# S5 state-space mix with a gated feed-forward: x's last 1024 tokens turned in 32 by 32 blocks on VectorE, parameters loaded on ScalarE's queue

## The chip, the cores and the metric

One core of one Trainium2 chip. The metric is the device time of one execution in microseconds (us), median of several runs. Engines are named TensorE (PE in the profile; PEld its weight loads), VectorE (DVE), ScalarE (ACT), GpSimd (POOL) and SyncE (SP); SP, ACT and POOL can issue DMA transfers.

## The reference: what is computed

x is one sequence of 2048 tokens with 448 features, all in bf16.

```python
g = sigmoid((x * gate_w).sum(-1, keepdims=True))
# a: a diagonal state-space layer, complex state of 448
Lam_bar = exp(exp(log_dt) * Lam)
Bu = einsum("bld,pd->blp", x, ((Lam_bar - 1) / Lam)[:, None] * Bmat)
h[t] = Lam_bar * h[t-1] + Bu[t]
a = 2 * einsum("blp,dp->bld", h, Cmat).real + x * Dskip
# b: a feed-forward, 448 -> 1792 -> 448
b = silu(x @ w1) @ w2
out = g * a + (1 - g) * b
```

## The kernel before

**Tiles.** The tokens go in four chunks of 512 (`tc`). For each chunk TensorE makes the "x products": 14 tiles F (x times w1, 128 of the 1792 columns each) and 7 tiles B (x times B, real and imaginary parts of the state in seven slots of 128 rows). Both need x turned, features on the partitions, in `xT`. The 448 features are held in four blocks of 128 rows that start at features 0, 128, 256 and 320, so the third and the fourth overlap by 64; the products take halves of 64 rows from them, two tiles at a time on the two halves of the array (`x_products`, L647; the matmul is L663).

**Turning x.** TensorE turns x by transposes against an identity into PSUM, and VectorE ("d") or ScalarE ("a") evicts it: chunk 0 in `x0_transposes` (L468), chunks 1 to 3 in `x_transposes` (L498): 32 transposes (L508) and two evictions of 128x1024 each. Chunk 1 is evicted "da", chunks 2 and 3 "aa" (L874, L879).

**The lanes.** The recurrence is made real by turning each state with its own angle (tables COS and SIN): `lanes(tc)` (L706) on VectorE multiplies the B products (U, in the tiles UG) by COS and SIN into H, runs seven scans along the 512 tokens (L736) into Gf, gets these as bf16 back into UG (by POOL's transfers, in the last chunk by ScalarE, L746), turns them back and leaves the result in H0 to H3 (L766, a subtraction). Each chunk starts from the last column of the one before. H3 is the last chunk's; before that its space holds B as loaded (`Bnat`), until `b_transposes` (L593) has turned it.

**Readouts.** `readout` (L786) multiplies H of 128 tokens by the weights CP (L795); VectorE adds the rest (L798) and SP stores it. `ffn2` (L768) makes the second feed-forward product (L774); ScalarE scales it (L780) and POOL adds it by a transfer.

**Parameters.** `parameters` (L529): three rows (log_dt, Lambda's parts) are loaded into `prm`, copied on VectorE (L538), turned by TensorE (L536), evicted (L540); POOL makes the exponential (L543), VectorE the angles from L544 on, and from these COS and SIN with ScalarE.

**What sets the order.** `Plan.order` (L104) schedules all operations by costs and priorities that the kernel gives them: TensorE keeps the written order, the other engines take whichever ready operation has the lowest priority number. `Waits` (L204) then makes one fixed list for each engine. Loads stand on SP's queue in the written order (xn0's first half, w1, the parameters, B, the last of w1, gate_w, Dskip, chunk 1 of x, w2, C, chunks 2 and 3 of x); ScalarE's queue has xn0's second half and two transfers of w1. w1's columns come in four cuts; of each cut, the feature blocks 0 to 2 and the overlapping block 3 are separate transfers (`load_w1`, L394). At the end the kernel's order is written out in L864 to L883: x products of all chunks, and between and behind them `ffn2` (G) and `readout` (C); the last are G(12..15), then C(12..15), which read H3.

Of the kernel before, what the change touches and what calls it, by code (L numbers as in the profile page):

```python
# [11 lines left out]
BF16 = DT.bfloat16  # L12
# [10 lines left out]
NOT = 5  # L23
NWARM = 6
NFILL = 2
XCOL = [0, 128, 256, 320]

TURN = 6.283184
# [248 lines left out]
def bass_gated_mix__ssm_conv_s5__dense_activation_silu__prompt_kernel(nc, A_x, A_Lambda_re, A_Lambda_im, A_B_re, A_B_im, A_C_re, A_C_im,  # L277
               A_log_dt, A_Dskip, B_x, B_w1, B_w2, gate_w, out):
    with ExitStack() as ctx:
# [3 lines left out]
        def sb(name, shape, dtype):  # L283
            return E(nc.sbuf_tensor(name, list(shape), dtype))
# [1 line left out]
        x2, out2 = A_x[0], out[0]  # L286

        xnat = sb("xnat", [128, NTB, D_MOD], BF16)
        xT = sb("xT", [128, 4, S_TOK], BF16)
        w1s = sb("w1s", [128, 4, F_FF], BF16)  # L290
        w2s = sb("w2s", [128, NFB, D_MOD], BF16)
        BT = sb("BT", [128, 4, 896], BF16)
# [94 lines left out]
        def load(q, dst, src, name, nbytes, prio=None, after=()):  # L387
            nl[0] += 1
            prio = nl[0] if prio is None else prio
            P.add(q, lambda e: e.dma_start(dst, src), list(after), name.split(), 0.6 if q == "pool" else 0.5, prio, sem(), nbytes, tag="ld " + name)  # L390
# [3 lines left out]
        def load_w1(q, k, a, b):  # L394

            cols = slice(w1cuts[k], w1cuts[k + 1])
            src = B_w1[320:448, cols] if a == 3 else B_w1[128 * a:128 * b, cols].rearrange("(b p) f -> p b f", p=128)
            load(q, w1s[:, 3, cols] if a == 3 else w1s[:, a:b, cols], src, " ".join(f"w1_{k}_{i}" for i in range(a, b)),
                 256 * (b - a) * (cols.stop - cols.start))

        for h, q in enumerate(("sp", "act")):
            load(q, xnat[:, 2 * h:2 * h + 2, :], x2[256 * h:256 * h + 256, :].rearrange("(b p) d -> p b d", p=128), f"xn0{h}", 256 * 896)
        load_w1("sp", 0, 0, 2)
        load_w1("act", 0, 2, 3)
        load_w1("act", 0, 3, 4)
        for k in range(1, len(w1cuts) - 2):
            load_w1("sp", k, 0, 3)
            load_w1("sp", k, 3, 4)
        for k, v in enumerate((A_log_dt, A_Lambda_re, A_Lambda_im)):
            load("sp", prm[k:k + 1, 0:448], v.rearrange("(o n) -> o n", o=1), f"prm{k}", 896)  # L410
        Bnat = H[3][:, :, 0:D_MOD]
        load("sp", Bnat[:, 0:3, :], A_B_re[0:384, :].rearrange("(b p) d -> p b d", p=128), "H3_0 H3_1 H3_2", 384 * 896)
        load("sp", Bnat[0:64, 3, :], A_B_re[384:448, :], "H3_3", 64 * 896)
        load("sp", Bnat[64:128, 3, :], A_B_im[384:448, :], "H3_3i", 64 * 896)
        load("sp", Bnat[:, 4:7, :], A_B_im[0:384, :].rearrange("(b p) d -> p b d", p=128), "H3_4 H3_5 H3_6", 384 * 896)
        btn = {s: [f"BT{s}_{h}" for h in range(2)] for s in range(7)}
        load_w1("sp", len(w1cuts) - 2, 0, 3)
        load_w1("sp", len(w1cuts) - 2, 3, 4)
        for dst, src, name in ((gwb, gate_w, "gwb"), (dkb, A_Dskip, "dkb")):
            load("sp", dst[:, :], src.rearrange("(o n) -> o n", o=1).partition_broadcast(128).rearrange("p o n -> p (o n)"),  # L420
                 name, 128 * 896)
# [46 lines left out]
        def x0_transposes(q0, part, who):  # L468

            tk = Ps(2)  # L470

            def mm(pe):
                for q in (q0, q0 + 1):
                    for k in range(2):
                        o = ((q - q0) * 2 + k) * 64
                        for h in range(2):
                            p = slice(64 * h, 64 * h + 64)
                            r = pe.transpose(bk(tk, h).bitcast(BF16)[:, o:o + 64], xnat[p, 2 * part + k, XCOL[q]:XCOL[q] + 128], ident[p, p])  # L478
                return r
            PE(mm, [f"xn0{part}", "ident"], [tk], 4 * 0.054, "xT0")  # L480
            for h in range(2):
                src = lambda h=h: bk(tk, h).bitcast(BF16)[:, 0:256].rearrange("p (q b n) -> p q b n", q=2, n=64)
                dst = xT[:, q0:q0 + 2, 256 * part:256 * part + 256].rearrange("p q (b h n) -> p q b h n", h=2, n=64)[:, :, :, h, :]
                names = [f"xT0_{q}{part}{h}" for q in (q0, q0 + 1)]
                if who[h] == "d":
                    DVE(lambda e, src=src, dst=dst: e.tensor_copy(dst, src()), [tk], names, 0.28, 0, "xTe")  # L486
                else:
                    ACT(lambda e, src=src, dst=dst: e.activation(dst, src(), AF.Copy), [tk], names, act_cost(256), 0, "xTe")
# [4 lines left out]
        x0_transposes(2, 1, "dd")  # L493

        xn_of = {tc: {q: [f"xT{tc}_{h}" for h in range(2)] for q in range(4)} for tc in range(1, NCH)}
        xn_of[0] = {q: [f"xT0_{q}{part}{h}" for part in range(2) for h in range(2)] for q in range(4)}

        def x_transposes(tc, who):  # L498

            tk = Ps(2)  # L500

            def mm(pe):
                for q in range(4):
                    for b in range(4):
                        o = (q * 4 + b) * 64
                        for h in range(2):
                            p = slice(64 * h, 64 * h + 64)
                            r = pe.transpose(bk(tk, h).bitcast(BF16)[:, o:o + 64],  # L508
                                             xnat[p, 4 * tc + b, XCOL[q]:XCOL[q] + 128], ident[p, p])
                return r  # L510
            PE(mm, [f"xn{tc}", "ident"], [tk], 16 * 0.035, f"xT{tc}")
            for h in range(2):
                src = lambda h=h: bk(tk, h).bitcast(BF16).rearrange("p (q b n) -> p q b n", q=4, b=4)
                dst = xT[:, :, tc * CH:(tc + 1) * CH].rearrange("p q (b h n) -> p q b h n", h=2, n=64)[:, :, :, h, :]
                if who[h] == "d":
                    DVE(lambda e, src=src, dst=dst: e.tensor_copy(dst, src()), [tk], [f"xT{tc}_{h}"], 0.69, 2.2, "xTe")
                else:
                    ACT(lambda e, src=src, dst=dst: e.activation(dst, src(), AF.Copy), [tk], [f"xT{tc}_{h}"], act_cost(1024), 2.2, "xTe")

        cosn = [f"COS{k}" for k in range(4)] + ["COSd"]  # L520
        sinn = [f"SIN{k}" for k in range(4)] + ["SINd"]
# [101 lines left out]
        def evict(pair, tk):  # L623

            kinds = [t[0] for t in pair]
            for k, n in ((0, 2),) if pair[0][:2] == pair[-1][:2] and len(pair) == 2 else ((0, 1), (1, 1))[:len(pair)]:
                kind, tc, a = pair[k]
                step = pair[k + 1][2] - a if n == 2 else 1
                sl = slice(a, a + step * (n - 1) + 1, step)
                names = [t[2] for t in pair[k:k + n]]  # L630
                src = (lambda: bk2(tk)) if n == 2 else (lambda k=k: bk(tk, k)[:, None, :])
                if kind == "F":
                    dst = aT[tc % 2][:, sl, :]
                    ACT(lambda e, src=src, dst=dst: e.activation(dst, src(), AF.Silu),  # L634
                        [tk, "tbl"], [f"aT{tc % 2}_{m}" for m in names], act_cost(512 * n), 2.5, "silu")
                    continue
                U, un = UG[tc % 2], f"U{tc % 2}_"
                dst = U[:, sl, :]
                if tc == 0:
                    DVE(lambda e, src=src, dst=dst: e.tensor_copy(dst, src()), [tk], [f"{un}{m}" for m in names], 0.15 + 0.53 * n, 2.6, "U")  # L640
                else:
                    ACT(lambda e, src=src, dst=dst: e.activation(dst, src(), AF.Copy), [tk], [f"{un}{m}" for m in names], act_cost(512 * n), 5, "U")  # L642
                if 3 in names:
                    load("pool", U[0:64, 7, :], U[64:128, 3, :], un + "7a", 65536, 9, [un + "3"])
                    load("pool", U[64:128, 7, :], U[0:64, 3, :], un + "7b", 65536, 9, [un + "3"])

        def x_products(tiles, fill={}, wait=()):  # L647
# [10 lines left out]
            def steps(k, h, a, z):  # L658
                def body(pe):
                    for n, cut in list(enumerate(part[h]))[a:z]:  # L660
                        for b, ((i, p0), tile) in enumerate(zip(cut, pairs[k])):
                            tc = tile[1]
                            r = pe.matmul(bk(toks[k], b), weights(tile, p0, p0 + 64, i), xT[p0:p0 + 64, i, tc * CH:(tc + 1) * CH],  # L663
                                          start=(h == 0 and n == 0), stop=(h == 1 and n == 2))
                    return r
                reads = [n for cut in part[h][a:z] for (i, _), tile in zip(cut, pairs[k])
                         for n in xn_of[tile[1]][i] + (w1n(tile[2], i) if tile[0] == "F" else btn[tile[2]])]
                return PE(body, list(dict.fromkeys(reads)), [toks[k]], (z - a) * PE_MM[512], f"{pairs[k][0][0]}{pairs[k][0][1]}")
# [192 lines left out]
        def C(*tbs):  # L861
# [3 lines left out]
        NH = 8  # L865
        K = NH // 2
        x_products(F(0, 0, NH) + B(0) + F(0, NH) + B(1),
                   {(1, 0): [parameters], (K - 2, 0): turn_b[:1], K - 2: turn_b[1:2], K - 1: turn_b[2:], 7: xt(1, "da") + [lambda: lanes(0)]}, [K - 2])
        gates(0)
        gates(1)  # L870
        lanes(1)
        for f in cp(0) + G(0, 1) + cp(1, 2) + G(2, 3) + cp(3):
            f()
        x_products(F(1) + F(2, 0, 1) + B(2), {2: xt(2, "aa")})  # L874
        gates(2)
        lanes(2)
        for f in G(4, 5, 6, 7) + C(0, 1, 2, 3):
            f()
        x_products(F(2, 1) + B(3) + F(3), {1: xt(3, "aa"), 9: [lambda: gates(3), lambda: lanes(3)]})  # L879
        for f in C(4, 5, 6, 7) + G(8, 9, 10, 11):  # L880
            f()
        for f in C(8, 9, 10, 11) + G(12, 13, 14, 15) + C(12, 13, 14, 15):
# [36 lines left out]
```

## Time and profile before

| | us |
|---|---|
| median of 3 runs | 141.97 (141.42, 141.97, 142.10) |
| the profiled execution | 141.25 |
| its span | 139.5 |
| TensorE busy in the span | 135.9 |
| VectorE busy | 122.0 |
| ScalarE busy | 90.3 |
| mean granted TensorE clock | 0.998 |

The span is the time from the first to the last instruction of the program; 1.75 us of the execution lie around it. The profile lists each engine's busy time, the chain of work that ended last (followed back from the last instruction to what released it), and groups of instructions by source line with what ended the idle time before them. The timeline lists instructions in order of time: start, duration, engine, line, what it writes and reads. Consecutive instructions on VectorE overlap slightly, so the distance between starts, not the duration, is what one costs its engine.

### The profile page before, as it was taken

The numbers are of one execution on the slowest core, as the hardware profiler recorded it, in microseconds if no ns is written. First come the engines' busy times: TensorE is split into PE (matmuls) and PEld (weight loads), VectorE is DVE, ScalarE is ACT, GpSimd is POOL, SyncE is SP. The second block draws the span as 40 slices with busy tenths as digits, with TensorE's granted clock in tenths as the row PEclk, the third lists the DMA queues.
The fourth block names the chain that finished last, engine by engine and source line by source line (L and its number), as shares of the span: only waits on it lengthen the run. The fifth ranks groups of instructions, "written<-read, shape, count | busy, mean of one in ns | idle before, by whom it ended". The sixth has DMA issues, their size and how long they took to land.

```text
span 139.5 us, 3000 instructions
## 1 busy us (share of the span) xinstructions
PE 135.9 (97%) x1201; PEld 67.0 (48%) x1201; DVE 122.0 (87%) x179; ACT 90.3 (65%) x157; POOL 39.2 (28%) x72
## 2 busy tenths in 40 slices
PE   7999999999999999999999999999999999999992
PEld 2445454455544544455544544444455555555561
DVE  0319999999999999999999999999999999997053
ACT  3349768999989999823694887799931268312300
POOL 7134040100248440227733001824000314022220
PEclk9999999999999999999999999999999999999999
DMA  4998999510156770104976200674202322323242
GB/s 136 337 294 243 363 320 238 177 42 0 31 79 94 129 110 1 38 15 73 157 131 155 38 5 0 95 133 79 38 4 97 66 33 36 83 83 61 40 94 71
DMA packets 17956, 14.71 MB, mean 105 GB/s; under 512 B 2835, under 2 KB 17814, under 8 KB 17942
## 3 DMA queue, kind: packets, MB, share of 16 engines
q0 software_dynamic: 6064, 5.51, 24.8%
q1 hardware_dynamic: 11318, 8.65, 20.7%
q10 hardware_dynamic: 560, 0.36, 0.8%
q8 instruction: 9, 0.15, 0.4%
q14 instruction: 5, 0.04, 0.1%
HBM read 7.17 MB, written 1.84 MB: 65 GB/s over the span
## 4 chain that ended last, share of the span: by engine, by line
PE 97%; DVE 0%; issue 0%
PE ps L663 46%; PE ps L774 31%; PE ps L795 15%; PE ps L463 2%; PE ps L508 1%; PE ps L478 1%; PE ps L814 1%; PE ps L604 1%; DVE ot L798 0%; PE ps L675 0%; PE ps L464 0%; PE ps L536 0%
## 5 line engine op out<-in xcount | busy, mean ns | idle before, releaser
L663 PE MATMUL ps<-xT,w1s 64*128 64x512 bf16 x392 | 48.5, 378 | 0.0
L774 PE MATMUL ps<-w2s,aT 128*128 128x448 bf16 x224 | 43.2, 353 | 0.0
L634 ACT ACTIVATE aT<-ps 128x1024 bf16<-128x1024 f32 (+1 forms) x30 | 28.7, 969 | 8.5 <-PE ps L663 8.4
L774 PEld LDWEIGHTS ps<-w2s,aT 128*128 128x128 bf16 x224 | 21.7, 98 | 20.4 <-ACT xnat L849 0.4
L663 PEld LDWEIGHTS ps<-xT,w1s 64*128 64x128 bf16 x392 | 19.7, 94 | 22.3 <-DVE xT L486 0.7
L663 PE MATMUL ps<-xT,BT 64*128 64x512 bf16 x196 | 25.8, 376 | 0.0
L782 POOL DMA_DIRECT2D xnat<-fe x16 | 14.1, 900 | 37.9 <-ACT fe L780 37.2
L780 ACT ACTIVATE fe<-ps,g 128x448 bf16<-128x448 f32 x16 | 10.1, 632 | 21.1 <-PE ps L774 21.0
L390 POOL DMA_DIRECT2D UG<-Gf x27 | 14.7, 549 | 20.9 <-DVE Gf L736 20.4
L736 DVE TENSOR_TENSOR_SCAN Gf<-rc,gin,H 128x512 f32<-128x512 f32 x14 | 17.2, 1268 | 0.0
L795 PE MATMUL ps<-CP,H 128*128 128x448 bf16 (+2 forms) x98 | 16.4, 326 | 0.0
L663 PEld LDWEIGHTS ps<-xT,BT 64*128 64x128 bf16 x196 | 10.8, 94 | 11.1 <-DVE Gf L562 0.2
L798 DVE SCALAR_TENSOR_TENSOR ot<-ps,g,xnat 128x448 bf16<-128x448 f32 (+2 forms) x18 | 10.8, 622 | 6.0 <-issue 4.6
L390 POOL DMA_DIRECT2D UG<-UG x8 | 4.8, 597 | 29.2 <-ACT UG L642 17.4
L704 DVE TENSOR_TENSOR H<-UG,COS 128x3584 bf16<-128x3584 bf16 (+4 forms) x10 | 12.6, 1266 | 0.0
L795 PEld LDWEIGHTS ps<-CP,H 128*128 128x128 bf16 x98 | 8.9, 98 | 7.5 <-DVE k L752 0.4
L642 ACT ACTIVATE UG<-ps 128x1024 bf16<-128x1024 f32 (+1 forms) x12 | 10.7, 923 | 1.4 <-PE ps L663 1.4
L842 ACT ACTIVATE junk<-xg 128x448 bf16<-128x448 bf16 x16 | 9.2, 574 | 2.1 <-DVE xg L704 2.0
L849 ACT ACTIVATE xnat<-xnat,g 128x448 bf16<-128x448 bf16 x16 | 9.8, 671 | 0.2
L704 DVE TENSOR_TENSOR PI<-UG,SIN 128x512 bf16<-128x512 bf16 (+2 forms) x13 | 9.1, 722 | 0.0
L704 DVE TENSOR_TENSOR PO<-UG,SIN 128x1536 bf16<-128x1536 bf16 (+1 forms) x8 | 8.7, 1087 | 0.1
L736 DVE TENSOR_TENSOR_SCAN Gf<-rc,gin,H2C 128x512 f32<-128x512 f32 x7 | 8.5, 1265 | 0.0
(102 smaller groups left out, 126.5 us busy)
## 6 DMA issues: line engine op xcount, KB each, us to landing
UG<-Gf POOLq DMA_DIRECT2D x21, 128.0 KB, 2.5
xnat<-fe POOLq DMA_DIRECT2D x16, 112.0 KB, 2.6
out_dram<-ot SPq DMA_DIRECT2D x15, 112.0 KB, 1.7
w2s<-in_B_w_dram SPq DMA_DIRECT2D x1, 1568.0 KB, 11.8
xnat<-in_A_x_dram SPq DMA_DIRECT2D x3, 448.0 KB, 6.1
w1s<-in_B_w_dram SPq DMA_DIRECT2D x1, 576.0 KB, 6.2
UG<-UG POOLq DMA_DIRECT2D x8, 64.0 KB, 2.2
H2C<-in_A_C_re_dram SPq DMA_DIRECT2D x2, 196.0 KB
```

Source lines behind the costliest of these rows:

```text
L390: P.add(q, lambda e: e.dma_start(dst, src), list(after), name.split(), 0.6 if q == "pool" else 0.5, prio, sem(), nbytes, tag="ld " + name)
L634: ACT(lambda e, src=src, dst=dst: e.activation(dst, src(), AF.Silu), [tk, "tbl"], [f"aT{tc % 2}_{m}" for m in names], act_cost(512 * n), 2 ...
L642: ACT(lambda e, src=src, dst=dst: e.activation(dst, src(), AF.Copy), [tk], [f"{un}{m}" for m in names], act_cost(512 * n), 5, "U")
L663: r = pe.matmul(bk(toks[k], b), weights(tile, p0, p0 + 64, i), xT[p0:p0 + 64, i, tc * CH:(tc + 1) * CH], start=(h == 0 and n == 0), stop=( ...
L704: DVE(lambda e: e.tensor_tensor(o, a, b, op), r, w, dve_cost(n, 2), prio, tag)
L736: DVE(lambda e, s=s, b=b, init=init: e.tensor_tensor_scan(Gf[:, s, :], rc[:, b:b + 1].to_broadcast([128, CH]), A[:, s, :], init, ALU.mult, ...
L774: r = pe.matmul(bk(tk)[:, 0:D_MOD], aT[tc % 2][:, fb, o:o + 128], w2s[:, fb, :], start=(fb == 0), stop=(fb == NFB - 1))
L780: ACT(lambda e: e.activation(f[:, :], bk(tk)[:, 0:D_MOD], AF.Copy, scale=g1[:, tb:tb + 1]), [tk, f"g1_{tc}"], [fn], act_cost(448, 1), 7, "fe")
L782: P.add("pool", lambda e: e.dma_start(Tb[:, tb, :], f[:, :], accum_op=ALU.add), [fn, f"Tb{tb}"], [f"Tb{tb}"], 0.94, 2, sem(), 115000, tag= ...
L795: r = pe.matmul(bk(tk)[:, 0:b - a], H[tc][:, s, o:o + 128], CP[:, s, a:b], start=(s == 0), stop=(s == NSLOT - 1))
L798: DVE(lambda e, tk=tk, a=a, b=b: e.scalar_tensor_tensor(ot[tb % NOT][:, a:b], bk(tk)[:, 0:b - a], g[:, tb:tb + 1], Tb[:, tb, a:b], ALU.mul ...
L849: ACT(lambda e, tb=tb: e.activation(Tb[:, tb, :], xnat[:, tb, :], AF.Copy, scale=g[:, tb:tb + 1]), [f"xd{tc}", f"g_{tc}"], [f"Tb{tb}"], ac ...
```

## The change

The parameter rows go on ScalarE's queue, and `parameters` is placed after the first two half tiles of x products (`(0, 0)`) instead of the next two (`(1, 0)`). Each cut of w1 is loaded as blocks 0 and 1, and blocks 2 and 3 in one transfer, whose second block starts 64 rows after the first. `xT` is laid out by chunk. Chunks 2 and 3 of x are no longer turned on TensorE: VectorE turns them in 32 by 32 blocks from `xnat` into the space of H3 (X32, four instructions a chunk), and SP carries the blocks to their rows of `xT` in 16 transfers of 32 partitions by 16 runs of 32 elements. On VectorE, chunk 2 has priority 15 after `PI_5` (of lanes 0), chunk 3 has 20.5 after `H0_0`. `UDVE` names all seven slots, so that line changes nothing.

```diff
+XT1 = "da"
+XPRIO = {2: 15, 3: 20.5}
+XBLK = (2, 3)
+XBEH = {2: "PI_5", 3: "H0_0"}
+UDVE = (0, 1, 2, 3, 4, 5, 6)
...
-        xT = sb("xT", [128, 4, S_TOK], BF16)
+        xT = sb("xT", [128, NCH, 4, CH], BF16)
...
+            n = cols.stop - cols.start
+            if b == 4:
+                src = bass.AP(B_w1.tensor, 128 * a * F_FF + cols.start, [[F_FF, 128], [(320 - 128 * a) * F_FF, 2], [1, n]])
...
-        load_w1("act", 0, 2, 3)
-        load_w1("act", 0, 3, 4)
+        load_w1("act", 0, 2, 4)
         for k in range(1, len(w1cuts) - 2):
-            load_w1("sp", k, 0, 3)
-            load_w1("sp", k, 3, 4)
+            load_w1("sp", k, 0, 2)
+            load_w1("sp", k, 2, 4)
         for k, v in enumerate((A_log_dt, A_Lambda_re, A_Lambda_im)):
-            load("sp", prm[k:k + 1, 0:448], v.rearrange("(o n) -> o n", o=1), f"prm{k}", 896)
+            load("act", prm[k:k + 1, 0:448], v.rearrange("(o n) -> o n", o=1), f"prm{k}", 896, 5)
...
+        def x_blocks(tc):
+            X32 = H[3][:, 0:4, :].rearrange("p m (q b i) -> p m q b i", q=4, i=32)
+            names = [f"X32_{k}" for k in range(4)]
+            held = [f"H3_{s}" for s in range(7)] + ["H3_3i"]
+            turned = [f"BT{s}_{h}" for s in range(7) for h in range(2)]
+            xs = xnat[:, 4 * tc:4 * tc + 4, :]
+            for k, (q0, q1, c, b0, b1) in enumerate(((0, 3, 0, 0, 2), (0, 3, 0, 2, 4), (3, 4, XCOL[3], 0, 2), (3, 4, XCOL[3], 2, 4))):
+                n = q1 - q0
+                src = xs[:, b0:b1, c:c + 128 * n].rearrange("p b (q m i) -> p b q m i", q=n, i=32)
+                dst = X32.rearrange("p m q b i -> p b q m i")[:, b0:b1, q0:q1, :, :]
+                DVE(lambda e, dst=dst, src=src: e.transpose(dst, src), [f"xn{tc}", XBEH[tc]] + turned, [names[k]], 0.15 + 256 * n / 960, XPRIO[tc], "xTd")
+            k = sem()
+            for g in range(4):
+                for m in range(4):
+                    to = xT[32 * m:32 * m + 32, tc, :, :].rearrange("p q (b g i) -> p (q b) g i", b=4, i=32)[:, :, g, :]
+                    P.add("sp", lambda e, to=to, g=g, m=m: e.dma_start(to, X32[32 * g:32 * g + 32, m, :, :, :].rearrange("p q b i -> p (q b) i")),
+                          names + held, [f"xT{tc}_{g}{m}"], 0.66, 400, k, 32768, tag="xTm")
...
-                   {(1, 0): [parameters], (K - 2, 0): turn_b[:1], K - 2: turn_b[1:2], K - 1: turn_b[2:], 7: xt(1, "da") + [lambda: lanes(0)]}, [K - 2])
+                   {(0, 0): [parameters], (K - 2, 0): turn_b[:1], K - 2: turn_b[1:2], K - 1: turn_b[2:], 7: xt(1, XT1) + [lambda: lanes(0)] + [lambda: x_blocks(2)] * (2 in XBLK)}, [K - 2])
...
+        if 3 in XBLK:
+            x_blocks(3)
-        x_products(F(1) + F(2, 0, 1) + B(2), {2: xt(2, "aa")})
+        x_products(F(1) + F(2, 0, 1) + B(2), {2: xt(2, "aa")} if 2 not in XBLK else {})
...
-        x_products(F(2, 1) + B(3) + F(3), {1: xt(3, "aa"), 9: [lambda: gates(3), lambda: lanes(3)]})
+        x_products(F(2, 1) + B(3) + F(3), {1: xt(3, "aa") if 3 not in XBLK else [], 9: [lambda: gates(3), lambda: lanes(3)]})
```

More of the change, by code (lines that the diff above doesn't have):

```diff
@@ L396, in load_w1 @@
             cols = slice(w1cuts[k], w1cuts[k + 1])
-            src = B_w1[320:448, cols] if a == 3 else B_w1[128 * a:128 * b, cols].rearrange("(b p) f -> p b f", p=128)
-            load(q, w1s[:, 3, cols] if a == 3 else w1s[:, a:b, cols], src, " ".join(f"w1_{k}_{i}" for i in range(a, b)),
-                 256 * (b - a) * (cols.stop - cols.start))
+            n = cols.stop - cols.start
+            if b == 4:
+                src = bass.AP(B_w1.tensor, 128 * a * F_FF + cols.start, [[F_FF, 128], [(320 - 128 * a) * F_FF, 2], [1, n]])
+            else:
+                src = B_w1[128 * a:128 * b, cols].rearrange("(b p) f -> p b f", p=128)
+            load(q, w1s[:, a:b, cols], src, " ".join(f"w1_{k}_{i}" for i in range(a, b)), 256 * (b - a) * n)
         for h, q in enumerate(("sp", "act")):
@@ L416, in bass_gated_mix__ssm_conv_s5__dense_activation_silu__prompt_kernel @@
         btn = {s: [f"BT{s}_{h}" for h in range(2)] for s in range(7)}
-        load_w1("sp", len(w1cuts) - 2, 0, 3)
-        load_w1("sp", len(w1cuts) - 2, 3, 4)
+        load_w1("sp", len(w1cuts) - 2, 0, 2)
+        load_w1("sp", len(w1cuts) - 2, 2, 4)
         for dst, src, name in ((gwb, gate_w, "gwb"), (dkb, A_Dskip, "dkb")):
@@ L482, in x0_transposes @@
                 src = lambda h=h: bk(tk, h).bitcast(BF16)[:, 0:256].rearrange("p (q b n) -> p q b n", q=2, n=64)
-                dst = xT[:, q0:q0 + 2, 256 * part:256 * part + 256].rearrange("p q (b h n) -> p q b h n", h=2, n=64)[:, :, :, h, :]
+                dst = xT[:, 0, q0:q0 + 2, 256 * part:256 * part + 256].rearrange("p q (b h n) -> p q b h n", h=2, n=64)[:, :, :, h, :]
                 names = [f"xT0_{q}{part}{h}" for q in (q0, q0 + 1)]
@@ L495, in bass_gated_mix__ssm_conv_s5__dense_activation_silu__prompt_kernel @@
         xn_of = {tc: {q: [f"xT{tc}_{h}" for h in range(2)] for q in range(4)} for tc in range(1, NCH)}
+        for tc in XBLK:
+            xn_of[tc] = {q: [f"xT{tc}_{g}{m}" for g in range(4) for m in range(4)] for q in range(4)}
         xn_of[0] = {q: [f"xT0_{q}{part}{h}" for part in range(2) for h in range(2)] for q in range(4)}
@@ L513, in x_transposes @@
                 src = lambda h=h: bk(tk, h).bitcast(BF16).rearrange("p (q b n) -> p q b n", q=4, b=4)
-                dst = xT[:, :, tc * CH:(tc + 1) * CH].rearrange("p q (b h n) -> p q b h n", h=2, n=64)[:, :, :, h, :]
+                dst = xT[:, tc, :, :].rearrange("p q (b h n) -> p q b h n", h=2, n=64)[:, :, :, h, :]
                 if who[h] == "d":
@@ L638, in evict @@
                 dst = U[:, sl, :]
-                if tc == 0:
+                if tc == 0 and a in UDVE:
                     DVE(lambda e, src=src, dst=dst: e.tensor_copy(dst, src()), [tk], [f"{un}{m}" for m in names], 0.15 + 0.53 * n, 2.6, "U")
@@ L662, in body @@
                             tc = tile[1]
-                            r = pe.matmul(bk(toks[k], b), weights(tile, p0, p0 + 64, i), xT[p0:p0 + 64, i, tc * CH:(tc + 1) * CH],
+                            r = pe.matmul(bk(toks[k], b), weights(tile, p0, p0 + 64, i), xT[p0:p0 + 64, tc, i, :],
                                           start=(h == 0 and n == 0), stop=(h == 1 and n == 2))
```

## The prediction

> **What bounds the kernel now.** I read the chain of waits first, to see whose work sets the end.
>
> ```profile
> PE 135.9 (97%) x1201; PEld 67.0 (48%) x1201; DVE 122.0 (87%) x179; ACT 90.3 (65%) x157; POOL 39.2 (28%) x72
> ...
> DVE  0319999999999999999999999999999999997053
> ...
> PE 97%; DVE 0%; issue 0%
> ```
>
> TensorE is the chain from 0.76 us to 136.73 us. VectorE, though off the chain, has "9" in every slice from the fourth to the 36th: a second engine with no spare time, until shortly before the end. So I looked next at where the two meet: in the chain's pieces in order of time, and in VectorE's timeline.
>
> ```profile
> 5.00 3.82 PE ps L663 x30
> 8.82 0.18 PE ps L536 x4
> ...
> 45.55 0.47 PE ps L508 x32
> ...
> 77.23 0.47 PE ps L508 x32
> ...
> 120.79 10.59 PE ps L774 x56
> 131.38 5.35 PE ps L795 x42
> ```
>
> ```profile
> 124.07 2.09 DVE L704 TENSOR_TENSOR H<-UG,COS 128x2048 bf16<-128x2048 bf16 x2
> 126.07 2.09 DVE L704 TENSOR_TENSOR H<-H,PO 128x2048 bf16<-128x2048 bf16 x2
> 132.80 0.69 DVE L798 SCALAR_TENSOR_TENSOR ot<-ps,g,xnat 128x448 bf16<-128x448 f32 x1 [4.64 <-issue]
> ```
>
> The last four readouts (L795, at 131.38) read what the last lane chunk leaves in H3. VectorE finishes that at 128.16, so it is **3.2 us ahead** of TensorE, and this is all the slack it has: from 10.38 to 128.16 its timeline shows no gap above 0.15 us. Any work added to VectorE eats this slack; any work taken from TensorE eats it too.
>
> **Taken from TensorE.** x's chunks 2 and 3 lose their 32 transposes each: 2 x 0.47 = 0.94 us of the chain. TensorE would reach the last readouts at 131.38 - 0.94 = **130.44**. ScalarE loses the four evictions that belong to them (1.95 and 1.93 us), worth nothing: TensorE never waits for ScalarE in the chain.
>
> **The parameters come earlier.** Of VectorE's and ScalarE's beginning:
>
> ```profile
> 8.16 0.17 DVE L538 COPY prm<-prm 3x64 bf16<-3x64 bf16 x1 [2.84 <-DMA prm<-in_A_Lambda_im_dram]
> 9.04 0.17 DVE L540 COPY pc<-ps 128x12 f32<-128x12 f32 x1 [0.71 <-PE ps L536]
> ...
> 10.38 0.16 DVE L544 SCALAR_TENSOR_TENSOR ph<-dtc,pc 128x4 f32<-128x4 f32 x1 [0.88 <-POOL dtc L543]
> ```
>
> ```profile
> 1.25 0.97 ACTq L390 DMA_DIRECT2D w1s<-in_B_w_dram  x2
> 2.25 1.28 ACT L457 ACT_TABLE_LOAD   x1 [2.25 <-issue]
> 4.06 1.00 ACT L488 ACTIVATE xT<-ps 128x256 bf16<-128x256 bf16 x3 [0.53 <-PE ps L478]
> ```
>
> ScalarE's queue now issues one w1 transfer instead of two (half of 0.97) and three parameter rows; SP took 0.93 us for these (3.75 to 4.68). That ends at 1.25 + 0.5 + 0.93 = 2.68, the table load at 3.99, and x's first eviction waits for TensorE until 4.06 in any case: no cost, with 0.07 us left; past that, TensorE's start would move one for one. The rows land about 6.2 (before: 8.16, 3.5 us after their last issue). TensorE turns them after 16 products instead of 30: 14 x 3.82/30 = 1.78 us earlier, at 7.04, after the rows and their copy. So L544 starts at 8.60, not 10.38. Part of this is lost: the first turned B block leaves TensorE at 10.85 as before, and with 1.78 us more in hand VectorE idles about 0.3 us for it; the third pair of B products (18.1, from the products counted back from 19.64) costs about 0.1. I take a **head start of 1.35 us** for the lanes (1.0 if more such waits come, 1.78 at most). SP issues everything behind the rows 0.93 us earlier, which nothing waits for. w1 moves the same bytes in as many transfers on SP: 0.
>
> **Added to VectorE: eight 32 by 32 transposes**, per chunk two of 768 and two of 256 elements in each partition. No row of before shows this operation. Rows at one element a cycle are nearest, since each element is read and written once without arithmetic in pairs: 128x512 f32 subtract (L527) goes 13.10 to 13.70, 0.60 us to the next start; the 1024 eviction from PSUM (L640) 15.24 to 16.37, 1.13. That is 0.07 + 1.04 ns an element: 0.87 and 0.34, so 2.42 us a chunk and **4.84** for both. Bounds: at the copy's pace (L565, 1536 in 0.45, 0.29 ns) 1.7; at the scan's (L736, 512 in 1.19, 2.3 ns) 9.6. Behind the first chunk's blocks on VectorE stand the rest of lanes 0 and CP's evictions: CP0 comes about 0.9 us later than now, while its bank is wanted at 34.4 (ready 32.5); CP3 is ready at 42.8, wanted about 44. Neither stops TensorE. Behind the second stand all of lanes 1 to 3.
>
> **Sum.** H3 is ready at 128.16 - 1.35 + 4.84 = 131.65, against TensorE's 130.44: the 0.94 us is turned into a wait in front of the last readouts. With 0.1 us from one engine to the next they start at 131.75 instead of 131.38, **0.37 us late**, and what follows (5.35 us of products, last store) is as before. 141.25 of the profiled execution becomes 141.62. That execution is 0.72 us under the median of the runs shown (141.97), so I forecast on the median: **142.3**.
>
> **The transfers.** Per chunk 16 transfers of 32 KB on SP, in 64-byte pieces: 8192. The first chunk's blocks follow PI_5: lanes start 26.0, blocks run 29.6 to 33.2 around CP0. TensorE wants chunk 2 at 50.1 (92 products after 40.15). So 16 issues and their pieces have 14.9 us, with 2 us for the last to land (stores take 1.7). SP's issues take 0.42 to 0.82 us (two 512-piece loads in 1.65): 6.7 to 13.1. For the pieces: the trace's packets of 128 B on SP's queue take 13 ns, 8192/16 x 13 = 6.7 us; all packets of the window 19 to 25:
>
> ```profile
> DMA packets 2515, 1.50 MB, mean 250 GB/s; under 512 B 1036, under 2 KB 2482, under 8 KB 2514
> ...
> q1 hardware_dynamic: 2450, 1.35, 95.1%
> ```
>
> 0.951 x 16 x 6 us / 2450 = 37 ns, so 19 us. I take the 128-byte row, nearest in size: landed about 43 to 48, hidden. Chunk 3 starts about 62.5 and is wanted at 81; its last four transfers stand on SP behind the first three stores (70 to 73): landed about 76, hidden. Stores wait behind the transfers meanwhile; five buffers cover that until about 102.
>
> **Rivals.**
> 1. *The transposes don't overlap with the next instruction* (slower). If each costs its full duration, by L527's 0.68 for 512 a fixed 0.15: 8 x 0.15 + 4.27 = 5.5 us. H3 at 132.3, 1.0 us late: 142.3 on the profiled execution, **143.0** on the median. It decides from 5.2 us for the eight on. [...] Against: every row shown overlaps by 0.07 to 0.08. [...]
> 2. *The transposes are cheap, or the head start is whole* (faster). Under 3.5 us for the eight (some 0.8 ns an element) H3 is no longer late: all of 0.94 is gained, **141.0** on the median. For: L565's copy moves 0.29 ns an element. Against: it is a copy of rows in order.
> 3. *Chunk 2 lands late* (slower). Over about 28 ns a piece, or 0.93 us an issue, TensorE stalls at 50.1. Up to 1.2 us of it vanishes in the wait for H3. At 37 ns: 54.1, a 4.0 us stall, last readouts at 134.4, 3.1 us late: **145** on the median. Against: those 37 ns belong to packets of 551 B on the mean.
>
> That the order is not as the diff says is excluded: VectorE's and TensorE's lists of after show it.
>
> **Chances.** Forecast 0.47, rival 1 0.25, rival 2 0.13, rival 3 0.12; 0.03 for a small stall unnamed. The range, 141.0 to 143.9, holds the first three and what lies between, and leaves out most of rival 3. About 0.5% (0.7 us) is what a measurement can tell from no change: faster 0.13, the same 0.46, slower 0.41.
>
> **What would show it.** In after, no transposes of chunks 2 and 3 on TensorE; L544's counterpart near 8.6; lanes 0 from about 26.0; transposes near 0.9 and 0.4 us; VectorE's last H3 subtraction ending near 131.7 without the gap in front of the last stores' evictions; and TensorE idle about 1.3 us before its last readouts, put down to VectorE, with no wait for a transfer at 50 or 81. Wrong it would be by a wait at 50 (rival 3), or by no wait before the last readouts (rival 2).

## The result, and the profile after

| | before | after |
|---|---|---|
| median, measured side by side | 141.71 (141.23 to 142.52, 10 runs) | 142.85 (142.23 to 143.93, 10 runs) |
| the profiled execution | 141.25 | 142.23 |
| its span | 139.46 | 140.43 |
| H3 ready (VectorE) | 128.16 | 131.34 |
| first of the last readouts (TensorE) | 131.22 | 131.40 |
| last eviction ends (VectorE) | 137.10 | 137.29 |
| from there to the end of the span | 2.36 | 3.14 |

After takes 1.0088 [1.0064, 1.0111] times as long as before: slower by 0.9%, where I had forecast 0.37 us (0.3%). The median lies in the forecast's range (141.0 to 143.9), but the loss of 1.14 us is three times the forecast one. In this table a stage's time is the start of its first instruction, which for the last readouts is 0.16 us ahead of the chain's 131.38, because the records of consecutive matmuls overlap. The two profiled executions differ by 0.98 us, as the medians do by 1.14, so the traces can be compared term by term.

The page of after, engines and chain:

```profile
PE 134.8 (96%) x1137; PEld 66.1 (47%) x1137; DVE 126.7 (90%) x187; ACT 86.9 (62%) x153; POOL 38.6 (27%) x72
...
DVE  0369999999999999999999999999999999999560
...
PE 4%; DVE 0%; issue 0%
```

TensorE lost 64 instructions and 1.1 us, VectorE gained eight instructions and 4.7 us. VectorE is busy earlier (its third slice is a 6 and not a 1), and its 9s end in the 37th slice, not the 36th. The chain of before was TensorE from 0.76 us on; now it breaks off after 4%. Its pieces in order of time (start, us, what):

```profile
131.35 0.05 issue
131.40 5.52 PE ps L824 x42
136.92 0.02 issue
136.94 0.35 DVE ot L827
```

The waits name what stands in front of 131.40, and a second stop of TensorE at 21.66 (engine, line, what it waited for: us in total, times, longest; a third, of 0.3 us at 4.79, belongs to the start):

```profile
PE ps L824 <- DVE H L733: 0.7, 1, 0.7
PE ps L692 <- ACT xT L527: 0.3, 1, 0.3
```

The first is the wait that the forecast saw coming: VectorE's last subtraction into H3. VectorE's timeline (start, duration), the start of the lanes in before and then after:

```profile
27.51 0.68 DVE L704 TENSOR_TENSOR H<-UG,COS 128x1024 bf16<-128x1024 bf16 x1
```

```profile
25.69 0.68 DVE L733 TENSOR_TENSOR H<-UG,COS 128x1024 bf16<-128x1024 bf16 x1
...
29.24 1.83 DVE L541 STREAM_TRANSPOSE H<-xnat 128x768 bf16<-128x768 bf16 x2
31.00 0.64 DVE L856 SCALAR_TENSOR_TENSOR CP<-ps,sc1s,ct 128x448 bf16<-128x448 bf16 x1
...
32.15 0.76 DVE L541 STREAM_TRANSPOSE H<-xnat 128x256 bf16<-128x256 bf16 x2
32.83 0.38 DVE L733 TENSOR_TENSOR H<-H,PI 128x512 bf16<-128x512 bf16 x1
...
129.25 2.09 DVE L733 TENSOR_TENSOR H<-H,PO 128x2048 bf16<-128x2048 bf16 x2
132.99 0.68 DVE L827 SCALAR_TENSOR_TENSOR ot<-ps,g,xnat 128x448 bf16<-128x448 f32 x1 [1.65 <-issue]
```

Two transposes of 768 elements run from 29.24 to the next start at 31.00, 0.88 us each; two of 256 from 32.15 to 32.83, 0.34 us each: 2.44 us for chunk 2. Chunk 3's four run from 59.45 to 61.86, 2.41 us: 4.85 for both. The lanes start at 25.69 (before: 27.51), and the idle time in front of the last readouts' first eviction fell from 4.64 to 1.65 us. The transposes are near the forecast; the lanes started earlier than it said.

The second stop was not forecast. ScalarE's timeline, its half of chunk 1's eviction in before, and then after, at the start and around chunk 1:

```profile
20.17 1.02 ACT L518 ACTIVATE xT<-ps 128x1024 bf16<-128x1024 bf16 x1
```

```profile
2.96 1.28 ACT L464 ACT_TABLE_LOAD   x1 [2.96 <-issue]
4.26 0.94 ACT L495 ACTIVATE xT<-ps 128x256 bf16<-128x256 bf16 x3
...
19.89 0.71 ACT L592 ACTIVATE COS<-Gf,hpi 128x512 bf16<-128x512 f32 x1
20.50 1.01 ACT L527 ACTIVATE xT<-ps 128x1024 bf16<-128x1024 bf16 x1
```

Because the angles come earlier, one more COS now stands in ScalarE's list ahead of its half of chunk 1's eviction, which in before started at 20.17. TensorE had arrived 0.28 us earlier than before (chunk 1's transposes at 19.19, not 19.47) and waits for that eviction:

```profile
20.73 0.60 PE L692 MATMUL ps<-xT,w1s 64*128 64x512 bf16 x4
21.66 0.37 PE L692 MATMUL ps<-xT,w1s 64*128 64x512 bf16 x1 [0.33 <-ACT xT L527]
```

The record's 0.33 us of idle time cost 0.49 us from start to start, since records of matmuls overlap otherwise, here by 0.16 us: TensorE reaches C's turning at 28.35 instead of 28.14, having led by 0.28.

The largest part lies behind the last readout. SP's last stores, before and then after (start, duration of the issue; before's first row holds two issues, the second of which is the row below it):

```profile
137.01 0.92 SPq L801 DMA_DIRECT2D out_dram<-ot  x2
137.51 0.43 SPq L801 DMA_DIRECT2D out_dram<-ot  x1
```

```profile
137.21 0.45 SPq L830 DMA_DIRECT2D out_dram<-ot  x1
138.10 0.33 SPq L830 DMA_DIRECT2D out_dram<-ot  x1
```

Before issues the last three stores back to back (136.54, 137.01, 137.51). After has a hole of 0.44 us in front of the last one, 137.66 to 138.10, though its data has been ready since 137.29. Two issues that stand back to back have 0.04 us between them. Of the DMA queues, after shows in the stretch from 137.5 us to the end

```profile
q14 instruction: 1, 0.01, 1.3%
```

and before no such packet in its last 3.5 us. In the trace's DMA records it is one packet of 8 KB of program at 138.7 us that takes 593 ns. Over the whole run after has six of them, before five, its last at 127.2. One completion of the last store arrives at 140.03, the others by 139.64; in before the last comes at 139.06, 0.03 us behind the one ahead of it. So the last store is issued 0.81 us behind the last eviction (before: 0.41) and takes 1.93 us to its last completion (before: 1.55).

### The profile page after: what moved, and what is told of

Its sections match the earlier page's. It is cut to its first block, busy times and chain, and to the rows that moved or that the text cites. A ratio compares the mean times of both kernels' runs of the same rounds, so it can differ in the third digit from the quotient of the medians.

```text
span 140.4 us, 2910 instructions
## 1 busy us (share of the span) xinstructions
PE 134.8 (96%) x1137; PEld 66.1 (47%) x1137; DVE 126.7 (90%) x187; ACT 86.9 (62%) x153; POOL 38.6 (27%) x72
## 5 line engine op out<-in xcount | busy, mean ns | idle before, releaser
L692 PE MATMUL ps<-xT,w1s 64*128 64x512 bf16 x392 | 47.9, 376 | 0.3 <-ACT xT L527 0.3
L803 PEld LDWEIGHTS ps<-w2s,aT 128*128 128x128 bf16 x224 | 21.7, 98 | 20.4 <-ACT UG L671 0.4
```

The lines of the kernel that those rows point to most:

```text
L803: r = pe.matmul(bk(tk)[:, 0:D_MOD], aT[tc % 2][:, fb, o:o + 128], w2s[:, fb, :], start=(fb == 0), stop=(fb == NFB - 1))
```

## The experiments

**Theory A:** the forecast's own step (VectorE late for H3) costs about 0.2 us; the rest is SP's longer list of instructions, whose last 8 KB packet comes in just when the last store is to be issued. **Theory B:** the rest is due to VectorE, ScalarE or the recut of w1. Theory A can be tested without touching the change: by it, small transfers added to SP early on shift the point at which a packet comes. The "8 small" and "32 small" below are copies of 32x32 elements of `ident` into a scratch tile, in addition to all of the kernel's work; the other engines' lists stay the same.

**e1, the start alone.** Both chunks are turned on TensorE again; parameters and w1 as in after.

```diff
-XBLK = (2, 3)
+XBLK = ()
```

> Only the parameters' move and w1's transfers (XBLK empty: chunks 2 and 3 are turned on TensorE again). My theory: the loss of the whole change is VectorE's blocks turned into a wait for H3, plus 0.7 us behind the last store; neither is here. TensorE's start gains about 0.3 us and a stall of 0.3 us at 21.7 us (chunk 1's eviction on ScalarE, seen in the changed kernel) takes it back: 0.0 us against before, within 0.3. VectorE starts the lanes 1.8 us earlier and idles that much longer before the last stores' evictions. Rival (the earlier parameters themselves cost, by ScalarE's later table load): +0.3 to +0.6 us.

141.93, ratio 1.0018 [0.9996, 1.0040], an interval that includes no change. H3 is ready at 127.96, long before it is read, and the stop is there, at 21.76. By the start's gain of 0.28 in after and the stop's 0.49, 0.21 us slower; the medians differ by 0.22. That sum is an estimate, for the start's gain scatters: against before's trace, chunk 1's transposes start 0.28 us earlier in after, 0.18 earlier here, 0.16 later in e6 and 0.84 later in e2. Earlier parameters are worth nothing that can be seen where VectorE has slack, and they bring the stop with them.

**e2, chunk 2 alone.**

```diff
-XBLK = (2, 3)
+XBLK = (2,)
```

> Only chunk 2 in blocks (16 transfers), chunk 3 on TensorE. My theory (VectorE has 3.2 us of slack, which eight blocks overdraw and four do not): H3 is ready near 128.8 us, TensorE arrives near 130.8, so no wait before the last readouts; one chunk's 0.47 us is gained: -0.5 us against before, if the store's tail stays as in before. Rival (each chunk's transfers cost by themselves, through SP's queue or the memory): half of the whole change's loss, +0.5 us.

141.35, ratio 0.9967 [0.9949, 0.9986]: faster than before, by 0.3%. Its chain of waits again runs through TensorE to the end:

```profile
121.68 10.59 PE ps L803 x56
132.27 5.35 PE ps L824 x42
```

H3 is ready at 129.86, 2.2 us ahead. Both times are about 1 us later than I expected: the profiled execution took 142.17, 0.82 over the median, and its TensorE waits 0.46 us for w1 at 7.0. TensorE keeps what one chunk frees: with the start's gain of after, -0.45 - 0.28 + 0.49 = -0.24, an estimate; the medians differ by -0.36. So half of the change pays, and with the second half VectorE is late.

**e3, before with 32 small transfers.**

```diff
+                P.add("sp", lambda e, i=i: e.dma_start(scr[:, 32 * i:32 * i + 32], ident[0:32, 0:32]), ["ident"] + behind, [f"scr{i}"], 0.66, 400, ks, 2048)
...
+        small(16, 0, ["PI_5"])
...
+        small(16, 16, ["H0_0"])
```

> The kernel before, with 32 small transfers more on SP's queue (32x32 elements from the identity to a tile nobody reads), 16 behind PI_5 and 16 behind H0_0; all other engines keep their order. Theory A (the last 0.7 us of the changed kernel come from SP's longer instruction stream: one more 8 KB instruction packet at 138.7 us, a gap of 0.44 us before the last store, a straggling completion): +0.7 us with the same packet after 137 us. Theory B (the tail was scatter of one execution): 0.0 us, within 0.2.

142.07, ratio 1.0020 [0.9998, 1.0042]. A sixth packet appears, at 137.6; the third store from the end is issued behind a hole of 0.46 us, and the span ends 0.37 us later, 0.30 us of it behind the last eviction (2.66 us from there to the end, not 2.36). The direction is theory A's, the size half of what I expected of it: the hole falls two stores earlier, and no completion straggles. The interval includes no change, so by itself this run is weak.

**e4, after with 8 small transfers.**

```diff
-... 7: xt(1, XT1) + [lambda: lanes(0)] + [lambda: x_blocks(2)] * (2 in XBLK)}, [K - 2])
+... 7: xt(1, XT1) + [lambda: lanes(0)] + [lambda: x_blocks(2)] * (2 in XBLK) + [lambda: small(8, 0, ["PI_5"])]}, [K - 2])
```

> The changed kernel with 8 small transfers more on SP (six before chunk 2's transfers, two behind); all other engines keep their order. Theory A (SP's instruction stream crosses a fetch at the very end): the crossing moves some eight instructions earlier, to a time when SP waits for stores anyway; the tail's 0.7 us go: -0.7 us against the changed kernel, +0.3 us against before. Theory B: no change, +1.1 us against before.

141.89, ratio 1.0009 [0.9990, 1.0028]: eight transfers *more* than after, and 0.96 us less time by the medians. A packet comes at 107.7 and none after 129.5; SP's last two stores stand back to back again:

```profile
137.64 0.44 SPq L837 DMA_DIRECT2D out_dram<-ot  x1
138.13 0.43 SPq L837 DMA_DIRECT2D out_dram<-ot  x1
```

The wait for H3 (ready at 131.78), 0.75 us in front of the last readouts (131.84), is as in after; from the last eviction to the end of the span it takes 2.37 us, as in before. What is left of the change's effect is +0.13 us by the ratio, and the interval includes none.

**e5, after once more, with e6 to e8.** No edit.

> The changed kernel once more, for a second profile beside the next three. Theory A (SP's instruction stream crosses a fetch at the very end, 0.7 us): the packet of 8 KB near 138.7 us and a gap before one of the last stores come again; +1.0 us against before. Theory B (scatter of one execution): no such packet after 130 us, or it has no gap with it.

142.88, ratio 1.0093 [1.0063, 1.0122]. The packet is back at 138.9 (541 ns), the hole of 0.44 us in front of the last store, and a completion 0.26 us behind the others. It is a property of this kernel, not of one execution.

**e6, relief for VectorE.** As e4, with the third pair of chunk 0's B products turned out of PSUM by ScalarE.

```diff
-UDVE = (0, 1, 2, 3, 4, 5, 6)
+UDVE = (0, 1, 2, 3, 6)
```

> The changed kernel with the 8 small transfers and with the third pair of chunk 0's B products evicted by ScalarE, which idled 1.8 us for TensorE there, instead of VectorE. Theory (VectorE from the parameters to H3 is the bound): lanes 0 start 1.1 us earlier, H3 is ready 1.1 us earlier, the wait of 0.75 us before the last readouts goes: -0.5 us against before. Rival (ScalarE was the better place for nothing: chunk 1's x comes later from it and TensorE stalls longer than 0.35 us near 21.7): 0.0 us or above.

140.98, ratio 0.9957 [0.9931, 0.9983]: the lowest median of all, though its interval overlaps with e2's. VectorE's lanes start at 24.96, 1.14 us ahead of e4's 26.10; H3 is ready at 130.35, and the chain is TensorE's again:

```profile
120.53 10.59 PE ps L810 x56
131.12 5.34 PE ps L831 x42
```

Against e4 the wait of 0.75 us is gone: the last readouts start at 130.96, not 131.84, and the profiled executions differ by 0.89 us (141.01 and 141.90). TensorE's terms then stand alone: -0.92 for two chunks, +0.49 for the stop, and the start. In this trace the start is 0.16 us later than before's, so the readouts begin 0.26 us ahead of before's (131.22), and the profiled executions differ by 0.24 (141.25 before). The medians differ by 0.80 (141.78 before), for before's profiled execution is 0.53 under its median; with after's start the sum would be -0.71, an estimate. What the start is worth on the median, no run isolates.

**e11, e6 without the small transfers.**

```diff
-... 7: xt(1, XT1) + [lambda: lanes(0)] + [lambda: x_blocks(2)] * (2 in XBLK) + [lambda: small(8, 0, ["PI_5"])]}, [K - 2])
+... 7: xt(1, XT1) + [lambda: lanes(0)] + [lambda: x_blocks(2)] * (2 in XBLK)}, [K - 2])
```

> After with the third pair of chunk 0's B products evicted by ScalarE, without the eight small transfers: the instructions of all engines but SP are in the same order as in e6. Theory A (SP's instruction stream gets its last 8 KB packet just before the last store): the packet is back near 138, the last store starts 0.4 us behind the one before it, one completion straggles, and the time is 0.7 to 1.0 us above e6: 141.7 to 142.0. Rival (e6's 141.0 owes nothing to the small transfers): 141.0 again, within 0.3.

141.60, ratio 1.0004 [0.9981, 1.0027]: by the ratios 0.47% (0.67 us) above e6, a little less than the 0.7 to 1.0 that I expected. SP's last stores, and the queue in the stretch from 137.5 us on:

```profile
137.68 0.45 SPq L830 DMA_DIRECT2D out_dram<-ot  x1
138.56 0.34 SPq L830 DMA_DIRECT2D out_dram<-ot  x1
```

```profile
q14 instruction: 1, 0.01, 1.2%
```

The hole is there (138.13 to 138.56), the packet comes at 139.2, and a completion is 0.5 us late. Over all profiles, the four with a packet near the end (after, e3, e5, e11) have a hole in the row of stores, with the packet 0.6 us behind the hole's end; the nine others (before, e1, e2, e4, e6 to e10) have neither. From the last eviction to the end of the span these nine take 2.35 to 2.38 us, e3 2.66, and after, e5 and e11 3.02 to 3.26. The runs with 44 to 60 transfers on SP have five such packets, those with 76 to 87 have six; so six alone do no harm, but the place of the sixth does.

**e8, SP's cuts of w1 as before.** As e4, with blocks 0 to 2 and block 3 in separate transfers again on SP's queue; ScalarE's stays as in after.

```diff
...
-            load_w1("sp", k, 0, 2)
-            load_w1("sp", k, 2, 4)
+            load_w1("sp", k, 0, 3)
+            load_w1("sp", k, 3, 4)
...
```

> The changed kernel with the 8 small transfers, and SP's w1 transfers cut as before (blocks 0 to 2, block 3); ScalarE's queue as changed; all other engines keep their order. My forecast was no effect: the same as with the 8 small transfers alone, +0.1 us against before, within 0.25. Rival (the new cut lets the second cut of w1 land later; TensorE's gap near 6 us, 0.05 to 0.5 us in the profiles of the changed kernels and none in before): 0.3 us faster than that.

141.94 against e4's 141.89; ratios 1.0041 [1.0009, 1.0073] and 1.0009 [0.9990, 1.0028]. The medians agree to 0.05 us and the intervals overlap: the recut on SP is worth nothing that can be seen.

**e7 and e10, late parameters.** As e4, with the rows on SP's queue and placed at (1, 0), as in before; e10 is the same kernel again.

```diff
-            load("act", prm[k:k + 1, 0:448], v.rearrange("(o n) -> o n", o=1), f"prm{k}", 896, 5)
+            load("sp", prm[k:k + 1, 0:448], v.rearrange("(o n) -> o n", o=1), f"prm{k}", 896)
...
-                   {(0, 0): [parameters],
+                   {(1, 0): [parameters],
```

> The changed kernel with the 8 small transfers, but the parameters on SP's queue and behind two half tiles more, as before. Theory (the head start of 1.8 us pays for VectorE's blocks one for one): lanes 0 start near 27.5, H3 is ready near 133.2, the last readouts start 1.9 us later than before: +1.9 us against before (143.6). ScalarE turns chunk 1 ahead of the third COS again, so TensorE's stall near 21.7 goes, which buys nothing here. Rival (VectorE's chain has other slack): +0.1 to +0.7 us.

> The same kernel as e7 (parameter rows late and on SP's queue), to see an undisturbed profile, since e7 took 1 us more than the start of the lanes explains. First theory: in e7's profile TensorE stops 2.1 us at 43.4 for a bank that ScalarE's eviction of the feed-forward has to free, and that eviction waits for POOL's transfer of an earlier result into xnat, which VectorE had not multiplied yet; the stop returns here with 1 to 2 us, but it precedes a wait of 1.9 us for H3, so it costs nothing by itself: the time is set by VectorE (lanes start 2.3 us later than in e4, plus any idle time in VectorE's own list). Rival: the stop belongs to that one execution; then the sum of 2.3 us alone gives 144.2. Expected in either case: 144.6 us again, with VectorE's list of the start showing where the further 0.5 to 1 us comes from.

e7 took 144.68, ratio 1.0219 [1.0193, 1.0245]: 2.9 us over before, 1 us more than expected. The trace read here is that of e10: 144.97, ratio 1.0233 [1.0201, 1.0265]. Its lanes start at 27.82, 1.72 us after e4's, but H3 comes 2.95 us later (134.73). TensorE stops at 42.84, and VectorE stops twice later on. TensorE's, then VectorE's timeline of e10:

```profile
44.77 5.57 PE L699 MATMUL ps<-xT,w1s 64*128 64x512 bf16 x50 [1.94 <-ACT fe L816]
```

```profile
71.32 0.68 DVE L834 SCALAR_TENSOR_TENSOR ot<-ps,g,xnat 128x448 bf16<-128x448 f32 x1 [1.05 <-PE ps L831]
...
73.97 0.68 DVE L834 SCALAR_TENSOR_TENSOR ot<-ps,g,xnat 128x448 bf16<-128x448 f32 x1 [0.37 <-PE ps L831]
```

I had expected the stop of TensorE to cost nothing, as it precedes a longer wait for H3. That was wrong: it delays the first readouts, VectorE's list has their evictions (L834) in the middle of lanes 1, and VectorE idles 1.05 and 0.37 us in front of them, where e4 has one idle time of 0.19: 1.23 us more. With the 1.72 that makes 2.95, as measured. The early parameters are thus worth 3 us to this change, far more than the head start alone.

**e9, the stop at 21.7 removed.** As e6; the planner is told that chunk 1's transposes take 0.5 us less, and the eviction gets a higher priority, so that ScalarE has it ahead of the fourth SIN.

```diff
-            PE(mm, [f"xn{tc}", "ident"], [tk], 16 * 0.035, f"xT{tc}")
+            PE(mm, [f"xn{tc}", "ident"], [tk], 16 * 0.035 - 0.5 * (tc == 1), f"xT{tc}")
...
-... [tk], [f"xT{tc}_{h}"], act_cost(1024), 2.2, "xTe")
+... [tk], [f"xT{tc}_{h}"], act_cost(1024), 0.5 if tc == 1 else 2.2, "xTe")
```

> As e6 (third pair of B products evicted by ScalarE, eight small transfers), with a planner cost changed so that ScalarE turns out chunk 1's half (1024 elements) ahead of the fourth SIN instead of behind it. Theory (the 0.34 us stop of TensorE at 21.8 is ScalarE's order, and TensorE sets the end once H3 is early): the stop is gone, TensorE reaches the last readouts about 0.34 us earlier, near 130.6, H3 is ready at about 130.4 as in e6, and the time falls to about 140.7 us (e6: 140.98). Rival (VectorE's chain still sets the end): its order shifts by the moved eviction, H3 comes at 130.6 or later, TensorE waits for it again, and the time stays within 0.1 us of e6 or goes above it.

142.11, ratio 1.0029 [1.0008, 1.0050]: 1 us slower than e6 by the ratios. The stop is gone, as expected, but the rival holds, and by more than I had put it. VectorE's and then TensorE's timeline:

```profile
20.75 0.69 DVE L532 COPY xT<-ps 128x1024 bf16<-128x1024 bf16 x1 [0.33 <-PE ps L524]
...
42.69 0.68 DVE L863 SCALAR_TENSOR_TENSOR CP<-ps,sc1s,ct 128x448 bf16<-128x448 bf16 x1 [0.90 <-ACT ct L858]
```

```profile
132.16 2.06 PE L831 MATMUL ps<-CP,H 128*128 128x448 bf16 x10 [1.06 <-DVE H L740]
```

The new lists give VectorE 0.33 and 0.90 us of waiting for TensorE and ScalarE, and in this execution TensorE also waited 0.6 us at 6 us for a part of w1, ahead of the parameters. H3 is 1.75 us later than in e6 (132.10) and TensorE waits again. A stop of the engine that was the bound is not worth removing if the list of the other one gets holes for it.

## Where the prediction held and where it failed, step by step

The direction, the range and VectorE's part of the mechanism held; the end of the program did not. That the median came out near rival 1's 143.0 is chance: rival 1's cause, dear transposes, is not there.

**TensorE's 0.94 us: right.** From start to start, chunk 2 gives 0.45 and chunk 3 0.47.

**ScalarE's queue at no cost: the margin was overdrawn.** The table load starts at 2.96, not 2.68, and x's first eviction at 4.26, not 4.06. TensorE waits 0.29 us at 4.79 for an eviction of x, and its first product starts 0.12 us later (5.01, not 4.89). In this execution it made up for it: the same instructions from its first product to the first turned B block take 5.16 us instead of 5.57, and chunk 1's transposes start 0.28 us earlier. Before's trace has TensorE's weight loads idle there for x's eviction (0.70 us in front of 5.73) and for w1 (0.37 us in front of 6.24); after's names neither. But this scatters: the same instructions take 5.35 us in e5, the same kernel, and 5.58 in e4.

**Head start: mis-sized, harmlessly.** L573 stands at 8.59 (forecast 8.60), and the lanes gained 1.82 us, not 1.35: the waits that I had deducted did not come, or the list went round them. My upper bound, 1.78, was nearly the true value.

**Eight transposes: right.** 4.85 against 4.84, so rival 1 is out, and so is the cheap half of rival 2. The two sizes differ by 0.54 us for 512 elements, 1.05 ns an element, and leave 0.07 us fixed, nearly as in the two rows of before that the forecast took (0.07 + 1.04 ns an element). What it calls one element a cycle is the pace of these rows; no trace shows a cycle of VectorE. The records of chunk 2's pairs end 0.07 and 0.08 us behind the start of the next instruction (31.07 against 31.00, 32.91 against 32.83), so the transposes overlap with it as other rows do.

**H3 and the wait: right in kind, half in size.** 128.16 - 1.82 + 4.85 = 131.19; measured 131.34 (forecast 131.65), with one idle time of VectorE that I did not list, 0.28 us at 71.78, when it waits for TensorE. The last readouts start 0.06 us after H3. From start to start they are 0.18 us late, not 0.37, because the head start was larger. TensorE's wait there is 0.73 us in the records, not 1.31: H3 came earlier, and the stop at 21.7 had cost TensorE more than its lead.

**A stop that I didn't list.** I cost the earlier parameters as a gain for VectorE alone and did not go through ScalarE's list for what they would overtake. At 21.7 us that costs TensorE 0.49 us, more than its lead of 0.28. In after it is hidden in the wait for H3; without the wait, as in e6, it counts in full.

**Transfers: right.** No wait at 50 or 81. The records show SP issuing chunk 2's 16 transfers from 32.93 to 44.78, and the last pieces done at about 46; a 64-byte piece takes 11 ns. Rival 3 is out. The page's list of DMA issues (KB each, us to landing) has them as

```profile
xT<-H SPq DMA_DIRECT2D x32, 32.0 KB, 2.7
```

**"What follows (5.35 us of products, last store) is as before": this step failed.** The products and evictions are: VectorE's last one ends 0.19 us late, as the readouts began. Behind it before needs 2.36 us and after 3.14. The 0.78 us more are the later issue of the last store (0.40, the hole) and the straggling completion (0.38), and they belong to SP's stores. SP is the engine to which the change gives 29 more transfers to issue (76, not 47). I had priced these transfers by their issue time, which is hidden, and not by their length as a program. 0.19 and 0.78 are the 0.97 us by which the spans differ; without the second (e4) the time is 0.13 us over before by the ratio, under the 0.37 that was forecast.

That the added transfers bring the hole, the straggler and the time, and that shifting them takes all three away, is shown (after, e5 and e11 against e4 and e6). That the hole is SP asking for its next 8 KB of program is read from the packets' kind, size, number and time; no run isolates it, and the traces do not say whose program a packet holds.

## What to carry over

When work is moved to an engine that looks idle, count its instructions as well as its time: an engine that only issues transfers may still issue the very last one. When two engines are within a few microseconds of each other, price each move on both, with its place in the fixed lists, for a stop of the one comes back as a hole in the other (e10, e9). And a change that is slower as a whole may hold a faster half: chunk 2 alone took 0.3% less time than before, and the whole change 0.4% less once two edits had relieved VectorE and shifted SP's program (e6).

## What the runs showed of the hardware

- A program packet (8 KB, 0.47 to 0.65 us) near the end of SP's list goes with a pause of 0.43 to 0.46 us in its issues (after, e3, e5, e11) and, when it meets the last store, with a completion 0.26 to 0.5 us behind the others. Where the sixth packet comes earlier (e4, at 107.7 us), the end of the program takes 2.37 us again, as in before (2.36).
- A 32 by 32 transpose on VectorE (bf16) costs 0.88 us from start to start for 768 elements in each partition and 0.34 for 256 (after).
- Transfers inside SBUF in 64-byte pieces (after): 11 ns a piece, and SP issues one of 512 pieces in 0.63 to 1.04 us in chunk 2, up to 1.55 in chunk 3.
- TensorE's third half tile waits for w1 near 6 us in some executions and hardly in others (0.09 us in e5, the same kernel as after, which has none; 0.35 in e4, 0.46 to 1.04 in e2, e9, e11). The same instructions, from the first product to the first turned B block, take 5.16 us in after and 6.49 in e11, which is a part of the spread between runs.
